# FFN chunks that run on over the batches: 10 chunks of up to 512 tokens in place of 12, and one x tile for all batches

## Chip, cores and metric

The kernel runs on one core of a Trainium2 chip. The metric is the device time of one execution in microseconds. In one job the fast executions of the kernel before lay within 0.3% (187.84 to 188.35 us). Now and then one takes some 3.7 us longer (191.78 in place of 188.1 us) at the same granted clock, which is the share of TensorE's full speed that the profile records as given. Such a run is called slow here, and it is left out of every ratio; the medians quoted are of all runs. "Stream" below is a second measure of mine. It is read from the trace's records at nanosecond resolution, and runs from the start of the first FFN matmul of token 1088 (the 49th pg, a term explained below, of every program but one, which is named) to the start of the last matmul on TensorE.

## The reference

Polynomial-sketch attention over 4 batches, 4 heads, 1088 tokens and head size 32, and then a squared-ReLU feed-forward network (FFN) over all 4352 tokens; the code is shortened.

```python
def _attn_ref(q, k, v, S1, S2):
    # phi(x): the outer product of two 8-wide sketches of x -> 64 features
    q_p, k_p = phi(q), phi(k)
    kv = np.einsum('bhsf,bhsd->bhfd', k_p, v)
    z = np.sum(k_p, axis=2)
    num = np.einsum('bhsf,bhfd->bhsd', q_p, kv)
    den = np.einsum('bhsf,bhf->bhs', q_p, z)[..., None] + 1e-06
    return num / den

def _moe_ref(x, w_in, w_out):            # x: 4352 x 128, w_in: 128 x 2048
    h = np.maximum(x @ w_in, 0.0)
    return h * h @ w_out

# x = attention output, (batch, seq) x (head * head_dim)
```

## The kernel before

The attention of batch b+1 is woven into the FFN of batch b. The FFN goes over the tokens in chunks (`FC`, one list for each batch). For every chunk it goes through 16 slices of 128 hidden units. One slice is one first-layer matmul into a PSUM tile `pg`, a relu on ScalarE, a square on ScalarE or VectorE, and one second-layer matmul that accumulates into `po`. I call the pg of one slice with the po of an earlier slice, as TensorE runs them, a block.

```python
    AC = [[(0, 8), (8, 12), (20, 16)]] + [[(0, 4 * NT)]] * (B - 1)
    FC = [[(0, 256), (256, 384), (640, 448)]] + [[(0, 384), (384, 384), (768, 320)]] * (B - 2)
    FC += [[(0, 448), (448, 384), (832, 256)]]
    ...
    for b in range(B):
        for ci, (c0, n) in enumerate(FC[b]):
            ...
                units.append((b, ci, c0, n, d0, m))      # one unit: m slices of a chunk
    ...
    def ffn1(u, i):                                      # pg; w_in and xT are fp32r
        nc.tensor.matmul(
            st["pg", u][:, n * i : n * i + n],
            w_in[:, 128 * (d0 + i) : 128 * (d0 + i) + 128],
            st[b, "xT"][:, c0 : c0 + n],                 # one xT tile for each batch
        )
    def ffn2(u, i, xs=None):                             # po; w_o and g are fp32
        ...                                              # (the last chunk: token-major, tokens on the partitions)
            nc.tensor.matmul(po[0][:, 0:n], w, g, start=(d == 0), stop=(d == NB - 1))
```

The attention puts four kinds of inserts into TensorE's stream: the sketches `kc` and `qc`, the key-value sums `kvp`, and `nd`, which makes numerator and denominator of x.

```python
    def a_nd(b, i0, nb): ...
        for e in range(E):
            qp = st[b, "qp", i0, e]
            ch = [(c, h) for c in range(4) for h in range(H)]
            for c, h in ch:
                r, o = slice(32 * c, 32 * c + 32), 64 * h + 32 * e
                nc.tensor.matmul(nd[32 * h : 32 * h + 32, 512 * c : 512 * c + m],
                                 kv[r, o : o + 32], qp[r, m * h : m * h + m], ...)
    def a_x(b, i0, nb, x, k=2): ...                      # VectorE: xT = nd * bc
```

A planner in the program orders the work of every engine from estimated durations. The order of the FFN matmuls among themselves is fixed, po and pg in turn. Where an insert falls in it is up to the planner, and a parameter `lag` sets how long after its inputs it may fall.

```python
    PEL, M, T0 = 0.3, 5.0, 1.5
    O.add(("nd", b, i0), {"PE": ...}, ..., uses=qps + ..., rings=[("att", 1)], lag=PEL)
    ...
    seq = [x for u in range(LU) for x in pe1[u]]
    for u in range(NU):
        p, q_ = list(pe2[u]), list(pe1[u + LU]) if u + LU < NU else []
        while p or q_:
            seq += p[:1] + q_[:1]
            p, q_ = p[1:], q_[1:]
```

## Time and profile before

| | before |
|---|---|
| time, median of 3 runs | 188.1 us (187.9 to 188.18) |
| span of the profiled run, granted TensorE clock | 186.1 us, 0.998 |
| TensorE / ScalarE / VectorE busy | 97% / 80% / 63% |
| blocks from token 1088 on | 144: 5 chunks of 384, 2 of 320, 1 of 448, 1 of 256 (the last) |
| stream (token 1088 to the last matmul) | 124.258 us |

The page and the lists of waits that bound the kernel stand in the prediction. Durations of single matmul records are of little use, since they overlap: in the two FFN groups shown there, po is busy for 138.4 us and pg for 110.2, together more than the span.

### The profile page before, as it was taken

Reading aid. Unit: us, or ns where it says so; the run is one execution under the profiler, and the core shown is the slowest. Engines: PE = TensorE matmul, PEld = TensorE weight load, DVE = VectorE, ACT = ScalarE, POOL = GpSimd, SP = SyncE. Lnnn points to the kernel's source line nnn. Section 1 sums busy time; section 2 is a strip of 40 time slices with the busy share of each in tenths; the row PEclk is TensorE's granted clock in tenths of the full one; section 3 lists DMA queues with packets and bytes.
Section 4 is the critical chain, followed back from the end, with each engine's and each line's share of the span. In section 5 each row is a group of like instructions: output and inputs, shape, how many; then the busy total and the mean of one; then the engine's idle time right before and its main releaser. Section 6 shows DMA issues by size and latency. Waiting matters only on the chain.

```text
span 186.1 us, 4132 instructions
## 1 busy us (share of the span) xinstructions
PE 180.4 (97%) x1561; PEld 120.8 (65%) x1562; DVE 116.7 (63%) x263; ACT 149.3 (80%) x329; POOL 35.8 (19%) x157
## 2 busy tenths in 40 slices
PE   8998999999999999999999999999999999999991
PEld 2766766666555566666577666656577655666891
DVE  4979989958991699379934689379943412222400
ACT  3509778878979889789698989789698998999960
POOL 2736405327400000184000000185000000000000
PEclk9999999999999999999999999999999999999999
DMA  5899600100039600200059200200020200020200
GB/s 181 201 301 330 168 0 5 28 4 0 4 48 250 153 4 0 45 3 0 13 120 270 38 4 0 42 4 0 8 40 0 35 0 2 8 41 4 30 12 28
DMA packets 24555, 11.27 MB, mean 61 GB/s; under 512 B 17880, under 2 KB 23000, under 8 KB 24536
## 3 DMA queue, kind: packets, MB, share of 16 engines
q1 hardware_dynamic: 24084, 10.82, 24.5%
q8 instruction: 12, 0.20, 0.5%
q10 hardware_dynamic: 452, 0.20, 0.4%
q14 instruction: 7, 0.06, 0.1%
HBM read 8.78 MB, written 2.23 MB: 59 GB/s over the span
## 4 chain that ended last, share of the span: by engine, by line
PE 95%; DMA 2%; DVE 1%; ACT 0%; issue 0%; POOL 0%; ACTq 0%; DVEq 0%
PE po L619 60%; PE pg L581 18%; PE nd L531 3%; PE kvp L397 2%; PE pol L614 2%; PE po L614 2%; PE qc L299 2%; DMA s_nat<-in_S_dram 2%; PE kvp L379 1%; PE kf L309 1%; PE kc L299 1%; PE x L713 1%; ACT gt L590 0%; PE den L774 0%; PE num L774 0%
## 5 line engine op out<-in xcount | busy, mean ns | idle before, releaser
L619 PE MATMUL po<-g,w_o 128*128 128x384 f32 (+3 forms) x352 | 138.4, 478 | 0.0
L581 PE MATMUL pg<-xT,w_in 128*128 128x384 f32 (+3 forms) x192 | 110.2, 582 | 0.5 <-ACT gt L590 0.5
L590 ACT ACTIVATE gt<-pg 128x384 f32<-128x384 f32 (+4 forms) x177 | 85.3, 489 | 19.3 <-PE pg L581 16.1
L619 PEld LDWEIGHTS po<-g,w_o 128*128 128x128 f32 x352 | 62.5, 189 | 22.6 <-issue 7.4
L598 ACT ACTIVATE g<-gt 128x384 f32<-128x384 f32 (+3 forms) x138 | 70.9, 531 | 2.9
L581 PEld LDWEIGHTS pg<-xT,w_in 128*128 128x128 f32 x192 | 36.0, 189 | 25.0 <-issue 6.0
L600 DVE TENSOR_TENSOR g<-gt 128x384 f32<-128x384 f32 (+4 forms) x39 | 21.9, 563 | 38.4 <-ACT gt L590 38.4
L438 POOL COPY kv<-kvt 32x64 f32<-32x64 f32 x48 | 11.8, 246 | 71.3 <-PE po L619 63.0
L492 POOL COPY rd<-rc 32x9 f32<-32x9 f32 (+2 forms) x80 | 16.6, 207 | 13.2 <-DVE rc L484 9.9
L501 DVE STREAM_SHUFFLE qa<-qc 128x576 f32<-128x576 f32 (+2 forms) x20 | 11.6, 648 | 0.0
L516 DVE TENSOR_TENSOR qp<-qa,qb 128x576 f32<-128x576 f32 (+2 forms) x20 | 10.8, 600 | 0.0
L464 DVE STREAM_TRANSPOSE qt<-qc 128x576 f32<-128x576 f32 (+2 forms) x10 | 5.8, 615 | 6.2 <-PE qc L299 6.2
L350 DVE TENSOR_TENSOR kp<-fs 128x576 f32<-128x576 f32 x12 | 8.2, 741 | 0.0
L623 DVE STREAM_TRANSPOSE oT<-po 128x384 f32<-128x384 f32 (+3 forms) x11 | 6.1, 559 | 1.8 <-PE po L619 1.8
L531 PE MATMUL nd<-qp,kv 32*32 32x288 f32 (+2 forms) x320 | 6.8, 353 | 0.0
L341 DVE STREAM_TRANSPOSE fs<-kc 128x576 f32<-128x576 f32 x6 | 4.3, 762 | 3.2 <-PE kc L299 3.2
L550 DVE TENSOR_TENSOR xT<-nd,bc 128x576 fp32r<-128x576 f32 (+2 forms) x10 | 5.6, 600 | 1.0 <-PE nd L531 1.0
L531 PEld LDWEIGHTS nd<-qp,kv 32*32 32x32 f32 x320 | 3.8, 103 | 3.6 <-issue 1.7
L501 DVE STREAM_SHUFFLE qb<-qc 128x576 f32<-128x576 f32 (+2 forms) x10 | 6.0, 646 | 0.0
L541 DVE STREAM_TRANSPOSE bc<-rd 128x576 f32<-128x576 f32 (+2 forms) x10 | 5.8, 606 | 0.2
L292 DVE STREAM_TRANSPOSE qT<-qn 128x192 f32<-128x192 f32 (+3 forms) x11 | 5.8, 564 | 0.0
L614 PE MATMUL pol<-w_o,g 128*128 128x128 f32 x32 | 5.7, 275 | 0.0
(94 smaller groups left out, 94.1 us busy)
## 6 DMA issues: line engine op xcount, KB each, us to landing
kn<-in_k_dram SPq DMA_DIRECT2D x3, 544.0 KB, 6.3
qn<-in_q_dram SPq DMA_DIRECT2D x3, 544.0 KB, 6.7
vn<-in_v_dram SPq DMA_DIRECT2D x9, 144.0 KB, 5.3
out_dram<-oT SPq DMA_DIRECT2D x24, 48.0 KB, 1.8
w_in<-in_moe_w_in_dram SPq DMA_DIRECT2D x4, 256.0 KB, 5.6
w_o<-in_moe_w_out_dram SPq DMA_DIRECT2D x4, 256.0 KB, 6.5
out_dram<-oT SPq DMA_DIRECT2D x8, 56.0 KB, 1.9
vn<-in_v_dram SPq DMA_DIRECT2D x3, 112.0 KB, 6.1
```

The costliest lines, as they stand in the source:

```text
L350: nc.vector.tensor_tensor(out=_ap(st[b, "kp"], 0, 128, 2 * o, [[64, NT], [8, 8], [1, 8]]), in0=_ap(fs, 0, 128, o, [[32, NT], [1, 8], [0, 8]]),
L438: nc.gpsimd.tensor_copy(_ap(st[b, "kv"], 32 * c, 32, 64 * h, [[32, E], [1, 32]]), _ap(st["kvt"], 32 * h, 32, 0, [[64, E], [1, 32]]),)
L492: nc.gpsimd.tensor_copy(st[b, "rd", i0][32 * h : 32 * h + 32, n * c : n * c + n], st["rc"][32 * c : 32 * c + 32, n * h : n * h + n],)
L501: nc.vector.stream_shuffle(in_=banks(st[b, "qc", i0], 2 * x, 0, m), out=_ap(st[b, which, i0], 0, 128, 2 * m * x, [[m, 2], [1, m]]), mask=m ...
L516: nc.vector.tensor_tensor(out=st[b, "qp", i0, e][:, r], in0=st[b, f"qa{e}", i0][:, r], in1=st[b, "qb", i0][:, r], op=mult,)
L531: nc.tensor.matmul(nd[32 * h : 32 * h + 32, 512 * c : 512 * c + m], kv[r, o : o + 32], qp[r, m * h : m * h + m], start=(e == 0), stop=(e = ...
L581: nc.tensor.matmul(st["pg", u][:, n * i : n * i + n], w_in[:, 128 * (d0 + i) : 128 * (d0 + i) + 128], st[b, "xT"][:, c0 : c0 + n],)
L590: nc.scalar.activation(gt[:, 0:w], st["pg", u][:, 0:w], Relu)
L598: nc.scalar.activation(g2[:, 0:w], gt[:, 0:w], Square)
L600: nc.vector.tensor_tensor(out=g2[:, 0:w], in0=gt[:, 0:w], in1=gt[:, 0:w], op=mult)
L614: nc.tensor.matmul(po[x // 128][:, 0:128], g[:, x : x + 128], w, start=(d == 0), stop=(d == NB - 1),)
L619: nc.tensor.matmul(po[0][:, 0:n], w, g, start=(d == 0), stop=(d == NB - 1))
```

## The change

Its intent is to run fewer, wider blocks. Chunks no longer stop at a batch's end, so that five of them can have 512 tokens, the width of the program's PSUM tiles; for this the x of all batches has to lie in one tile. The core of the diff:

```diff
-    FC = [[(0, 256), (256, 384), (640, 448)]] + [[(0, 384), (384, 384), (768, 320)]] * (B - 2)
-    FC += [[(0, 448), (448, 384), (832, 256)]]
+    FC, at = [], 0
+    for n in (256, 384, 448, 448, 512, 512, 512, 512, 512, 256):
+        FC.append((at, n))
+        at += n
...
+    xT = sb("xT", B * S + SP - S, F32R)
...
-            out=_ap(st[b, "xT"], 0, 128, 32 * i0 + 2 * m * x, [[m, k], [1, m]]),
+            out=_ap(xT, 0, 128, S * b + 32 * i0 + 2 * m * x, [[m, k], [1, m]]),
...
-            st[b, "xT"][:, c0 : c0 + n],
+            xT[:, c0 : c0 + n],
...
-    def f_out(b, c0, n):
+    def f_out(c0, n):                      # a chunk across a boundary: two stores
+        for b in range(B):
+            lo, hi = max(c0, b * S), min(c0 + n, b * S + S)
...
-            ("x", b, i0, x) for i0, k in AC[b] for x in range(2)
-            if 32 * i0 + 16 * k * x < c0 + n and c0 < 32 * i0 + 16 * k * x + 16 * k
+            ("x", b, i0, x) for b in range(B) for i0, k in AC[b] for x in range(2)
+            if b * S + 32 * i0 + 16 * k * x < c0 + n
+            and c0 < b * S + min(32 * i0 + 16 * k * x + 16 * k, S)
```

The rest of the diff drops the batch index from units, tiles and task names.

More of the change, by code (lines that the diff above doesn't have):

```diff
@@ L547, in a_x @@
         m = 8 * nb
-        if (b, "xT") not in st:
-            st[b, "xT"] = bpool.tile([128, SP], F32R, tag="xT", name="xT")
         nc.vector.tensor_tensor(
-            out=_ap(st[b, "xT"], 0, 128, 32 * i0 + 2 * m * x, [[m, k], [1, m]]),
+            out=_ap(xT, 0, 128, S * b + 32 * i0 + 2 * m * x, [[m, k], [1, m]]),
             in0=banks(st[b, "nd", i0], 2 * x, 0, m, k),
@@ L558 @@
     units, first_unit, dur = [], {}, []
-    for b in range(B):
-        for ci, (c0, n) in enumerate(FC[b]):
-            first_unit[b, c0] = len(units)
-            nb = 512 // n
-            sizes = [nb] * (NB // nb)
-            if (b, ci) == (0, 0):
-                sizes = [1, 1] + [2] * 7
-            d0 = 0
-            for m in sizes:
-                units.append((b, ci, c0, n, d0, m))
-                dur.append(m * (5 * n / 2400 + 0.015))
-                d0 += m
+    for ci, (c0, n) in enumerate(FC):
+        first_unit[c0] = len(units)
+        nb = 512 // n
+        sizes = [nb] * (NB // nb)
+        if ci == 0:
+            sizes = [1, 1] + [2] * 7
+        d0 = 0
+        for m in sizes:
+            units.append((ci, c0, n, d0, m))
+            dur.append(m * (5 * n / 2400 + 0.015))
+            d0 += m
     NU = len(units)
-    last = len(FC[B - 1]) - 1
+    last = len(FC) - 1
     g2s = {}
     def ffn1(u, i):
-        b, ci, c0, n, d0, m = units[u]
+        ci, c0, n, d0, m = units[u]
         if i == 0:
@@ L583, in ffn1 @@
             w_in[:, 128 * (d0 + i) : 128 * (d0 + i) + 128],
-            st[b, "xT"][:, c0 : c0 + n],
+            xT[:, c0 : c0 + n],
         )
     def relu(u):
-        w = units[u][3] * units[u][5]
+        w = units[u][2] * units[u][4]
         gt = fpool.tile([128, 512], F32, tag="gt", bufs=GT, name="gt")
@@ L593, in square @@
     def square(u, eng):
-        w = units[u][3] * units[u][5]
+        w = units[u][2] * units[u][4]
         g2 = fpool.tile([128, 512], F32, tag="g2", bufs=G2, name="g2")
@@ L603, in ffn2 @@
     def ffn2(u, i, xs=None):
-        b, ci, c0, n, d0, m = units[u]
+        ci, c0, n, d0, m = units[u]
         d = d0 + i
         if d == 0:
-            st["po", b, c0] = [psf.tile([128, 512], F32, tag="po", name="po")]
-            if (b, ci) == (B - 1, last):
-                st["po", b, c0].append(att("pol"))
-        po = st["po", b, c0]
+            st["po", c0] = [psf.tile([128, 512], F32, tag="po", name="po")]
+            if ci == last:
+                st["po", c0].append(att("pol"))
+        po = st["po", c0]
         g, w = g2s[u][:, n * i : n * i + n], w_o[:, 128 * d : 128 * d + 128]
-        if (b, ci) == (B - 1, last):
+        if ci == last:
             for x in range(0, n, 128) if xs is None else xs:
@@ L619, in ffn2, with f_oT, f_last @@
             nc.tensor.matmul(po[0][:, 0:n], w, g, start=(d == 0), stop=(d == NB - 1))
-    def f_oT(b, c0, n):
-        oT = fpool.tile([128, 448], F32, tag="oT", bufs=2, name="oT")
-        nc.vector.transpose(oT[:, 0:n], st["po", b, c0][0][:, 0:n])
-        st["oT", b, c0] = oT
-    def f_out(b, c0, n):
-        for dm in range(4):
-            nc.sync.dma_start(
-                bass.AP(
-                    out.tensor, out.offset + (b * S + c0 // 32) * 128 + 32 * dm,
-                    [[G * 128, 32], [128, n // 32], [1, 32]],
-                ),
-                _ap(st["oT", b, c0], 32 * dm, 32, 0, [[32, n // 32], [1, 32]]),
-            )
-    def f_last(b, c0):
-        po = st["po", b, c0]
+    def f_oT(c0, n):
+        oT = fpool.tile([128, 512], F32, tag="oT", bufs=2, name="oT")
+        nc.vector.transpose(oT[:, 0:n], st["po", c0][0][:, 0:n])
+        st["oT", c0] = oT
+    def f_out(c0, n):
+        for b in range(B):
+            lo, hi = max(c0, b * S), min(c0 + n, b * S + S)
+            if lo >= hi:
+                continue
+            i0, m = (lo - b * S) // 32, (hi - lo) // 32
+            for dm in range(4):
+                nc.sync.dma_start(
+                    bass.AP(
+                        out.tensor, out.offset + (b * S + i0) * 128 + 32 * dm,
+                        [[G * 128, 32], [128, m], [1, 32]],
+                    ),
+                    _ap(st["oT", c0], 32 * dm, 32, lo - c0, [[32, m], [1, 32]]),
+                )
+    def f_last(c0):
+        po, b = st["po", c0], B - 1
         def store(eng, i):
@@ L641, in store @@
                 bass.AP(
-                    out.tensor, out.offset + (b * S + c0 // 32 + 4 * i) * 128,
+                    out.tensor, out.offset + (b * S + (c0 - b * S) // 32 + 4 * i) * 128,
                     [[128, 4], [G * 128, 32], [1, 128]],
@@ L798 @@
     nc.vector.transpose(bc0[:, :], _ap(rd0, 0, 128, 0, [[1, 8], [0, 32]]))
-    st[0, "xT"] = bpool.tile([128, SP], F32R, tag="xT", name="xT")
     nc.vector.tensor_tensor(
-        out=st[0, "xT"][:, 0:256], in0=num0[:, 0:256], in1=bc0[:, :], op=mult
+        out=xT[:, 0:256], in0=num0[:, 0:256], in1=bc0[:, :], op=mult
     )
@@ L809, with unit_at @@
         t += 1.14 * dur[u]
+    def unit_at(x):
+        return first_unit[max(c for c, _ in FC if c <= x)]
     def due(b, c0):
-        c = max(c for c, _ in FC[b] if c <= c0)
-        return tu[first_unit[b, c]] - LA
+        return tu[unit_at(b * S + c0)] - LA
     def dve(n):
@@ L901, in nd_tasks @@
                 uses=[("bc", b, i0, x), ("nd", b, i0)],
-                rings=[("xT", 2)] if x == 0 and (i0 == 0) else [],
             )
@@ L912, in k_tasks @@
     def k_tasks(b, k0, ks_lead):
-        s0 = tu[first_unit[b - 1, 0]] - 4.0 if b > 1 else 0.0
+        s0 = tu[unit_at(b * S - S)] - 4.0 if b > 1 else 0.0
         O.add(
@@ L985 @@
     for u in range(NU):
-        b, ci, c0, n, d0, m = units[u]
+        ci, c0, n, d0, m = units[u]
         w = n * m
         xt = [
-            ("x", b, i0, x) for i0, k in AC[b] for x in range(2)
-            if 32 * i0 + 16 * k * x < c0 + n and c0 < 32 * i0 + 16 * k * x + 16 * k
+            ("x", b, i0, x) for b in range(B) for i0, k in AC[b] for x in range(2)
+            if b * S + 32 * i0 + 16 * k * x < c0 + n
+            and c0 < b * S + min(32 * i0 + 16 * k * x + 16 * k, S)
         ]
@@ L1023 @@
         pe2.append(mm2s)
-        if d0 + m == NB and (b, ci) != (B - 1, last):
-            po = [x for u_ in range(first_unit[b, c0], u + 1) for x in pe2[u_]]
-            O.add(("oT", b, c0), {"DVE": dve(n)}, tu[u] + 3.0, [], on(f_oT, b, c0, n), uses=po,
+        if d0 + m == NB and ci != last:
+            po = [x for u_ in range(first_unit[c0], u + 1) for x in pe2[u_]]
+            O.add(("oT", c0), {"DVE": dve(n)}, tu[u] + 3.0, [], on(f_oT, c0, n), uses=po,
                   rings=[("oT", 2)])
             O.add(
-                ("out", b, c0), {"SP": 2.0}, tu[u] + 4.0, [], on(f_out, b, c0, n),
-                uses=[("oT", b, c0)],
+                ("out", c0), {"SP": 2.0}, tu[u] + 4.0, [], on(f_out, c0, n),
+                uses=[("oT", c0)],
             )
@@ L1043 @@
     O.run()
-    f_last(B - 1, FC[B - 1][last][0])
+    f_last(FC[last][0])
 _INS = ['q', 'k', 'v', 'S1', 'S2', 'moe_w_in', 'moe_w_out']
```

## The prediction

> **What bounds the kernel now.** I read the page's busy shares and chain first, then TensorE's waits, then the timeline of TensorE in steady stretches of the three chunk widths, then ScalarE and VectorE around the places that the change touches.
>
> ```profile
> PE 180.4 (97%) x1561; PEld 120.8 (65%) x1562; DVE 116.7 (63%) x263; ACT 149.3 (80%) x329; POOL 35.8 (19%) x157
> ...
> PE 95%; DMA 2%; DVE 1%; ACT 0%; issue 0%; POOL 0%; ACTq 0%; DVEq 0%
> ...
> L619 PE MATMUL po<-g,w_o 128*128 128x384 f32 (+3 forms) x352 | 138.4, 478 | 0.0
> L581 PE MATMUL pg<-xT,w_in 128*128 128x384 f32 (+3 forms) x192 | 110.2, 582 | 0.5 <-ACT gt L590 0.5
> ```
>
> TensorE is 95% of the chain that ended last, and the two FFN lines almost never find it idle: 0.0 and 0.5 us. The list of TensorE's waits says the same in full:
>
> ```profile
> PE warm L662 <- PEq L1058: 0.8, 1, 0.8
> PE pg L581 <- ACT gt L590: 0.5, 1, 0.5
> PE kf L309 <- ACT sq L683: 0.3, 1, 0.3
> PE qc L299 <- issue: 0.3, 1, 0.3
> ```
>
> 1.9 us in four waits, all within the first 16 us, which the change leaves alone. So a saving on ScalarE, VectorE or the queues is worth nothing; only what TensorE's own stream costs counts. Records of a pipelined matmul overlap, so I take that cost from the starts of the same instruction in consecutive blocks. A block is one first-layer matmul (pg) and the second-layer ones (po) of an earlier block:
>
> ```profile
> 67.14 0.63 PE L581 MATMUL pg<-xT,w_in 128*128 128x384 f32 x1
> ...
> 75.34 0.63 PE L581 MATMUL pg<-xT,w_in 128*128 128x384 f32 x1
> ...
> 134.53 0.55 PE L581 MATMUL pg<-xT,w_in 128*128 128x320 f32 x1
> ...
> 142.08 0.55 PE L581 MATMUL pg<-xT,w_in 128*128 128x320 f32 x1
> ...
> 146.79 0.71 PE L581 MATMUL pg<-xT,w_in 128*128 128x448 f32 x1
> ...
> 156.32 0.71 PE L581 MATMUL pg<-xT,w_in 128*128 128x448 f32 x1
> ```
>
> Between the two lines of a pair lie 10, 11 and 10 blocks: 0.820, 0.686 and 0.953 us a block at 384, 320 and 448 columns. From 320 to 448 that is 2.086 ns a column, and what is left at zero columns is 0.686 - 320 x 0.002086 = 0.0185 us (0.019 from the 384 row). **A block costs about 0.019 us whatever its width, the rest is proportional to the columns.**
>
> **What the Trainium skill says.** "TensorE: Matmul & The Clock Gate", section "Wait — 56ns, not 53.3ns?", gives a warm back-to-back matmul as N / 2.4 GHz plus a fixed 2.5 ns or so. "FP8 and Floating Point Precision", section "TensorE Precision Notes", has four passes for true fp32. The trace agrees in form: 2.086 ns a column is five passes at 2.4 GHz (2.083), one for pg, whose operands are the reduced fp32r type, and four for the fp32 po. In size the fixed part is larger here, 19 ns for three records, against 7.5 ns if it were 2.5 each; I use the trace. "PSUM — Partial Sum Buffer", section "The four PSUM rules", limits a matmul's output to one bank, 512 fp32 columns. So 512 is the end of this road; the tiles pg and po are allocated 512 wide already, so no buffer count changes. "ScalarE: Activation LUTs", section "What ACT_TABLE_LOAD costs", gives an ACTIVATE with immediate operands 186 ns + 0.833 ns a column, with back-to-back ones overlapping by 93 ns. The trace's 481 ns at 384 and 588 ns at 512 columns are 0.836 ns a column and 160 ns fixed, for relu out of PSUM; squares have 0.859 and 190. No page bears on the scheduling.
>
> **The change part by part.**
>
> Common part. The instruction order of both programs is the same on TensorE until the first pg of token 1088, at 57.68 us: the 256-, 384- and 448-column chunks of batch 0 are unchanged. Nothing changes there.
>
> Fewer blocks. From token 1088 on, before has per 16 blocks: five chunks of 384, two of 320, one of 448, one of 256 (the last, which is computed token-major in both). After has one of 448, five of 512, one of 256. The same 3264 columns in 144 blocks against 112. At 512 columns a block is, extrapolated, 0.953 + 64 x 0.002086 = 1.0865 us. Before: 16 x (5 x 0.820 + 2 x 0.686 + 0.953) = 102.8 us. After: 16 x (0.953 + 5 x 1.0865) = 102.2 us. The exact difference is 32 blocks x about 0.0195 = **-0.63 us**, all of it on the path.
>
> Attention inserts. The matmuls of batches 2 and 3 (kc, kvp, qc, nd) stay the same in number and shape, but three of them move from between pg and po to between po and pg. Read by pg starts, an insert between po and pg looks dearer: kvp costs 2.46 - 0.82 = 1.64 us at 37.08 to 39.54, against 2.27 - 0.82 = 1.45 us at 75.34 to 77.61. That would be +0.6 us for three and eat the whole gain. But the pg record that follows an insert is 0.44 us long instead of 0.63: its start is drawn later. By ends, 37.71 to 39.98, it is 2.27 - 0.82 = 1.45 us as well. So I put **0** here.
>
> ScalarE and VectorE. 177 relus become 145. Squares go from 138 on ScalarE and 39 on VectorE to 123 and 22. ScalarE records then sum to 2 x 0.38 + 16 x 0.481 + 32 x 0.534 + 95 x 0.588 = 81.4 us of relu and 16 x 0.520 + 28 x 0.573 + 79 x 0.630 = 74.1 us of square: 155.5 against 156.2 us before. Beside TensorE, **0**.
>
> Output. oT is transposed 9 times instead of 11, and the two chunks across a batch boundary are stored in two parts: still 44 stores from it. A store's landing is awaited by nobody before the end, and the last chunk is the same. **0**.
>
> Sum: 188.1 - 0.63 = **187.5 us**.
>
> **The rivals.**
>
> (a) x comes too late. A chunk across a boundary needs batch 2's x 128 tokens earlier and batch 3's 192 tokens earlier, some 4 and 6.5 us at 34 ns a token (0.820 x 16 / 384). The nd matmuls must therefore run earlier, and they wait for VectorE. In the kernel before the margin is small:
>
> ```profile
> 121.16 0.77 PE L299 MATMUL qc<-qT,sw 32*32 32x288 f32 x32
> ...
> 132.45 1.60 PE L531 MATMUL nd<-qp,kv 32*32 32x288 f32 x64
> ```
> ```profile
> 129.17 2.74 DVE L516 TENSOR_TENSOR qp<-qa,qb 128x576 f32<-128x576 f32 x4
> 131.84 1.43 DVE L541 STREAM_TRANSPOSE bc<-rd 128x576 f32<-128x576 f32 x2
> ```
>
> qp is done at 131.91, 9.98 us after qc's end and 0.54 us before nd. In the changed order ten po and nine pg of 512 columns stand between qc and nd of batch 3, an estimated 10 x 0.869 + 9 x 0.217 = 10.6 us; for batch 2 some 10.5 us. No other VectorE work is put in between. So the 0.5 us margin holds, and six or seven blocks (6.5 us or more) lie between nd and the first pg that needs the x, which takes VectorE 1.5 us. If the chain slipped by an unforeseen square (0.67 us) at both batches, the cost would be up to 0.3 us: 187.8. For it: the margin is thin. Against: the counts.
>
> (b) ScalarE becomes the bound. Two relus and two squares at 384 take 1.50 us at their closest (87.76 to 89.26), 0.75 a unit; 128 more columns add 0.22: 0.97 against 1.087 on TensorE. Where a square directly follows its own relu, 66.17 to 67.12 shows 0.95 a unit, so 1.17 at 512: ScalarE falls back 0.08 us a unit there, against 0.13 before. The longest such stretch is some nine units, 0.7 us, with a lead of about 1.3 us by the two pg buffers, and inserts let it catch up. If it bit, +0.5 to 1 us: 188 to 188.5.
>
> (c) One x tile for all batches makes false waits: a pg that reads batch 1's tokens waiting for the write of batch 2's, 1 to 2 us at each of two boundaries, 189 to 191. The listing of the changed program's waits speaks against it: the pg after nd wait for ScalarE alone, and the first that waits for VectorE is the one that needs the new x.
>
> (d) The fixed part is not per block but a hidden weight load, and 512 columns gain nothing: 188.1. The equal remainder at three widths speaks against it.
>
> **Range and chances.** The gain is certain in sign if nothing new waits, and 0.3% in size; a slip of (a) or (b) could take it back, (c) hardly. The three times before span 0.28 us. I say 187.5, with 187.0 to 188.1 for 8 in 10. A change over 2% needs 3.8 us, six times what I can find in either direction: 0.01 faster, 0.97 within, 0.02 slower.
>
> **What would show it.** Right: pg starts 1.087 us apart at 512 columns; TensorE's waits still under 2 us and only at the start; the first 256-column pg of the last chunk 0.6 us earlier than before's 170.76 us; nd of batches 2 and 3 still a few tenths after qp. Wrong: a block at 512 over 1.10 us; a wait of nd for qp or of pg for the x or a relu; an insert between po and pg that costs more by record ends too.

## The result, and the profile after

| | before | after |
|---|---|---|
| time, median of all 4 runs | 188.14 us | 187.91 us |
| fast runs (one slow run of each left out) | 187.9 to 188.18 | 187.57 to 187.93 |
| ratio of fast runs, 95% interval | | 0.9986 (0.9963 to 1.0009) |
| stream | 124.258 us | 123.981 us |

A ratio here is the mean time of one kernel's fast runs over that of the other's fast runs in the same rounds, so it is not quite the ratio of the medians quoted. The change is worth 0.1 to 0.2%, and these rounds alone would not tell it from nothing. The stream is 0.277 us shorter; that I can read to some nanoseconds, because two traces of one program agree to that (shown below), while the start-up ahead of it shifts by tenths of a microsecond from run to run: the first FFN matmul started between 13.66 and 14.29 us in the traces. The two profiled runs both have a span of 186.1 us for that reason.

The page of the kernel after, first its line of busy times (time, share of the span, instructions), then the chain by engine, then the two FFN groups (busy, mean ns of one, idle before):

```profile
PE 180.5 (97%) x1466; PEld 105.0 (56%) x1466; DVE 109.6 (59%) x244; ACT 147.5 (79%) x282; POOL 35.6 (19%) x157
...
PE 94%; DMA 2%; DVE 1%; ACT 0%; issue 0%; POOL 0%; ACTq 0%; DVEq 0%
...
L620 PE MATMUL po<-g,w_o 128*128 128x512 f32 (+3 forms) x288 | 133.2, 546 | 0.1
L582 PE MATMUL pg<-xT,w_in 128*128 128x512 f32 (+3 forms) x160 | 104.6, 664 | 0.6 <-ACT gt L591 0.5
```

There are 32 blocks fewer, and TensorE bounds the kernel as before. Its busy time did not fall (180.4 to 180.5 us). Busy time joins overlapping records, so a stream without gaps is busy for as long as it lasts, and the 0.28 us that it lost are hidden by the start-up, where 12 warming matmuls ran in place of 11 (5.1 us against 4.5). Its waits in full (us in total, times, longest):

```profile
PE warm L668 <- PEq L1065: 0.8, 1, 0.8
PE pg L582 <- ACT gt L591: 0.5, 1, 0.5
PE kf L313 <- ACT sq L689: 0.3, 1, 0.3
```

All three are in the start-up, so no new wait ate the gain. The spacing of the blocks is what differs from the prediction. TensorE's timeline (start and length in us), on both sides of the nd of batch 3:

```profile
116.99 0.79 PE L582 MATMUL pg<-xT,w_in 128*128 128x512 f32 x1
...
124.60 0.79 PE L582 MATMUL pg<-xT,w_in 128*128 128x512 f32 x1
...
126.18 1.60 PE L535 MATMUL nd<-qp,kv 32*32 32x288 f32 x64
...
128.51 0.80 PE L582 MATMUL pg<-xT,w_in 128*128 128x512 f32 x1
...
139.44 0.80 PE L582 MATMUL pg<-xT,w_in 128*128 128x512 f32 x1
```

Seven blocks lie between the first two pg lines: 7.61 / 7 = 1.087 us, as predicted. Ten lie between the last two: 10.93 / 10 = 1.093 us. The same instructions on the same shapes cost 6.5 ns more each behind the nd than ahead of it, and the length of the pg record (0.79 or 0.80) is a handy mark of which spacing holds. From the records' starts, the 6.5 ns lie between the start of a pg and that of its first po record (630 against 636.5 ns); the other two gaps of a block are alike. A later weight load is not the cause: the load for that po starts 402 to 403 ns behind the pg and takes 190 ns in quick and slow blocks alike. Of the 67 steady 512-column blocks, 20 have 1.087 and 47 have 1.093: the slow ones are those behind the nd of batch 2 and of batch 3, up to the next insert or the end, and the others all run at 1.087.

Where the stream's time went, beyond what its columns take at 2.4 GHz (us; a part's records are counted end to end, less five passes a column at 1/2.4 ns):

| | before | after |
|---|---|---|
| ordinary FFN blocks | 127: 2.446 | 95: 2.168 |
| kc and qc (4) | 3.658 | 3.663 |
| kvp (2) | 2.944 | 2.946 |
| nd (2) | 3.491 | 3.515 |
| last chunk | 3.681 | 3.653 |

The ordinary blocks account for the -0.28 us; the rest cancels to within 0.01. At before's 19.3 ns a block, 95 blocks would have 1.83 us. The 0.34 us in between is 47 slow blocks at 6.7 ns, 0.31 us, and a few blocks where two widths meet.

### The profile page after: what moved, and what is told of

Same layout as the page of the kernel before. It is cut to its first block, busy times and chain, and to the rows that moved or that the text cites. A ratio compares the mean times of both kernels' runs of the same rounds, so it can differ in the third digit from the quotient of the medians.

```text
span 186.1 us, 3857 instructions
## 1 busy us (share of the span) xinstructions
PE 180.5 (97%) x1466; PEld 105.0 (56%) x1466; DVE 109.6 (59%) x244; ACT 147.5 (79%) x282; POOL 35.6 (19%) x157
## 4 chain that ended last, share of the span: by engine, by line
PE 94%; DMA 2%; DVE 1%; ACT 0%; issue 0%; POOL 0%; ACTq 0%; DVEq 0%
PE po L620 60%; PE pg L582 18%; PE nd L535 3%; PE kvp L401 2%; PE pol L615 2%; PE po L615 2%; DMA s_nat<-in_S_dram 2%; PE qc L303 2%; PE kvp L383 1%; PE kf L313 1%; PE kc L303 1%; PE x L719 1%; ACT gt L591 0%; PE warm L668 0%; PE num L780 0%
## 5 line engine op out<-in xcount | busy, mean ns | idle before, releaser
L620 PE MATMUL po<-g,w_o 128*128 128x512 f32 (+3 forms) x288 | 133.2, 546 | 0.1
L582 PE MATMUL pg<-xT,w_in 128*128 128x512 f32 (+3 forms) x160 | 104.6, 664 | 0.6 <-ACT gt L591 0.5
L591 ACT ACTIVATE gt<-pg 128x512 f32<-128x512 f32 (+3 forms) x145 | 81.0, 562 | 21.3 <-PE pg L582 20.5
L599 ACT ACTIVATE g<-gt 128x512 f32<-128x512 f32 (+2 forms) x123 | 71.9, 602 | 2.6
L620 PEld LDWEIGHTS po<-g,w_o 128*128 128x128 f32 x288 | 53.0, 189 | 30.1 <-issue 20.1
L582 PEld LDWEIGHTS pg<-xT,w_in 128*128 128x128 f32 x160 | 30.0, 189 | 31.3 <-issue 14.2
L601 DVE TENSOR_TENSOR g<-gt 128x512 f32<-128x512 f32 (+2 forms) x22 | 14.2, 649 | 41.8 <-ACT gt L591 41.8
L624 DVE STREAM_TRANSPOSE oT<-po 128x512 f32<-128x512 f32 (+3 forms) x9 | 5.9, 653 | 7.4 <-PE po L620 7.4
L668 PE MATMUL warm<-const-bfloat16-1.0 128*128 128x512 bf16 x12 | 5.1, 578 | 0.8 <-PEq L1065 0.8
```

Of the source, the lines that this page charges most:

```text
L582: nc.tensor.matmul(st["pg", u][:, n * i : n * i + n], w_in[:, 128 * (d0 + i) : 128 * (d0 + i) + 128], xT[:, c0 : c0 + n],)
L591: nc.scalar.activation(gt[:, 0:w], st["pg", u][:, 0:w], Relu)
L599: nc.scalar.activation(g2[:, 0:w], gt[:, 0:w], Square)
L601: nc.vector.tensor_tensor(out=g2[:, 0:w], in0=gt[:, 0:w], in1=gt[:, 0:w], op=mult)
```

## The experiments

Where a kernel ran once, I rely on its trace. All results were correct.

**Theory:** a 512-column block has two spacings, 6.7 ns apart, and which of them a stretch gets is settled when the stream restarts behind an insert. **Rivals:** the slow stretches are chance of the run; the fixed part of a block does not belong to the block at all (rival (d) of the prediction); the one x tile or the flat chunk list brings a cost of its own, which offset part of the gain.

### again: the changed kernel, unchanged

> The changed kernel once more. Block theory: TensorE's stream is shorter by 32 blocks x 20 ns = 0.64 us, less what the first trace shows to go against it: 53 of the 512-column blocks, all those between an nd and the next insert, came at 1.093 us apart and not 1.087, which is 53 x 6.7 ns = 0.35 us. Net -0.28 us, ratio 0.9985. If the slower spacing belongs to the program, the same blocks show it again; if it is luck of an execution, other blocks do, or none, and the ratio can be 0.9966.

Measured: 187.76 us against 188.06, ratio 0.9983 (0.9964 to 1.0002), in a later job. The stream is 123.981 us, to the nanosecond that of the first trace, though it begins 0.5 us later. Again 20 blocks have 1.087 and 47 have 1.093, in the same places. (The 53 of the expectation was a first count; 47 steady blocks are slow in both traces.) TensorE's timeline behind the nd of batch 3 in this run:

```profile
128.99 0.80 PE L582 MATMUL pg<-xT,w_in 128*128 128x512 f32 x1
...
136.64 0.80 PE L582 MATMUL pg<-xT,w_in 128*128 128x512 f32 x1
```

7.65 / 7 = 1.093 us. So the slow spacing belongs to the program and is not chance of the run.

### twelve: the old widths in the new form

```diff
-    for n in (256, 384, 448, 448, 512, 512, 512, 512, 512, 256):
+    for n in (256, 384, 448, 384, 384, 320, 384, 384, 320, 448, 384, 256):
```

> One x tile and the chunk list over all batches, but with the twelve widths of the kernel before. Block theory: 192 blocks as before, no chunk crosses a batch, ratio 1.000 within 0.001. Rival, that the one x tile itself makes or removes a wait: a ratio off 1.000 by 0.003 or more, and a wait of pg for VectorE in the trace.

Measured: 188.34 us against 188.06, ratio 1.0011 (0.9997 to 1.0025). The stream is 124.241 us against before's 124.258, and the 127 ordinary blocks have 2.463 us beyond their columns against 2.446. The one x tile and the flat list cost nothing on TensorE and give nothing: the rival of a hidden cost falls, and with it (c) of the prediction.

### eleven: 448 columns in place of 512

```diff
-    for n in (256, 384, 448, 448, 512, 512, 512, 512, 512, 256):
+    for n in (256, 384, 448, 448, 448, 448, 448, 448, 448, 320, 256):
```

> Eleven chunks of at most 448 columns, run on over the batches. Block theory: 16 blocks fewer than before, -0.32 us, ratio 0.9983, with 448-column blocks at 0.953 us everywhere. If crossing a batch costs something, a wait of nd for qp or of pg for xT shows at the chunks that cross. If the slower spacing after nd is not special to 512 columns, 448-column blocks of 0.960 us show after nd.

Measured: 188.13 us against 188.06, ratio 1.0002 (0.9988 to 1.0016). The stream is 124.069 us, 0.19 below before's. All 448-column blocks run at 0.953 us wherever they stand, behind an nd too, so the two spacings are seen at 512 columns alone. The ordinary blocks (111) have 2.173 us, as much as 95 blocks after the change: the slow spacing took almost exactly what the 16 blocks fewer were to give. One thing was not foreseen: the last chunk has 3.766 us here, 0.11 more than in the changed kernel. The trace shows where. The weight load of the pg behind the first token-major block starts 568 ns after the pg before it, against 451 in the changed kernel, and 52 ns after the end of a relu, which frees a pg buffer and which the profile names as what the load waited for. So TensorE waited there for ScalarE, in a gap that its list of waits does not show, because the records of the po before it cover it.

### fifteen: many narrow blocks

```diff
-    for n in (256, 384, 448, 448, 512, 512, 512, 512, 512, 256):
+    for n in (256, 384, 448, 256, 256, 256, 256, 256, 256, 256, 256, 256, 352, 352, 256):
```

> Fifteen chunks, nine of them of 256 columns: the same columns in 48 blocks more than before. Block theory: 48 x 20 ns = +0.96 us, ratio 1.0051, 256-column blocks at 0.553 us. Rival, that the fixed part is not paid per block: ratio 1.000. If 256-column blocks are bound by the three weight loads of a block: more than +2 us.

Measured: 188.38 us against 188.06, ratio 1.0013 (1.0000 to 1.0026); the stream is 124.308 us. With 20 ns for every block, 48 blocks more than before had to cost 0.96 us. The stream grew by 0.05. TensorE's timeline in a stretch of 256 columns:

```profile
106.08 0.47 PE L582 MATMUL pg<-xT,w_in 128*128 128x256 f32 x1
...
111.56 0.47 PE L582 MATMUL pg<-xT,w_in 128*128 128x256 f32 x1
```

Ten blocks in 5.48 us, 0.548 each (0.5467 by the records' starts). Five passes of 256 columns at 2.4 GHz are 0.5333, which leaves 13.3 ns, not 20. The 352-column blocks have 0.753 us, which leaves 20. And 144 x 13.3 + 32 x 20 = 2.56 us is what 128 blocks at 20 ns cost before. **A fixed part that is the same for every width falls here**, and this was the ground on which the prediction extrapolated to 512.

### nd_inside: the nd of batches 2 and 3 behind a pg instead of behind a po

```diff
-            uses=qps + [("qp", b, i0, 0, 0)], rings=[("att", 1)], lag=PEL,
+            uses=qps + [("qp", b, i0, 0, 0)], rings=[("att", 1)], lag=PEL + (0.6 if b > 1 else 0.0),
```

> The changed kernel with nd of batches 2 and 3 half a block earlier or later, between pg and po instead of between po and pg; nothing else moves by more than a block. Two traces of the changed kernel showed 1.093 us a 512-column block after such an nd and 1.087 after the other inserts. If the place of nd in the block sets the spacing: all 512-column blocks at 1.087 us, TensorE's stream from the 49th pg to the last matmul 0.35 us under 123.98 us, 123.63, and a ratio of 0.9966 to before. If nd itself sets it: 1.093 after nd again, 123.98 us, 0.9985.

Measured: 187.65 us against 188.25, ratio 0.9964 (0.9946 to 0.9981). The stream is 123.719 us, 0.54 below before's. TensorE's timeline behind the nd of batch 2 and behind that of batch 3:

```profile
87.63 1.60 PE L535 MATMUL nd<-qp,kv 32*32 32x288 f32 x64
...
89.72 0.80 PE L582 MATMUL pg<-xT,w_in 128*128 128x512 f32 x1
...
98.47 0.80 PE L582 MATMUL pg<-xT,w_in 128*128 128x512 f32 x1
...
126.36 1.60 PE L535 MATMUL nd<-qp,kv 32*32 32x288 f32 x64
...
128.45 0.79 PE L582 MATMUL pg<-xT,w_in 128*128 128x512 f32 x1
...
140.40 0.79 PE L582 MATMUL pg<-xT,w_in 128*128 128x512 f32 x1
```

8.75 / 8 = 1.094 us in the first pair, 11.95 / 11 = 1.086 in the second. Only the eight blocks behind the nd of batch 2 are slow now; the 38 behind that of batch 3, which reach to the last chunk, are not. TensorE's work is the same, and only the two inserts have moved, by one matmul each. Elsewhere the planner gave ScalarE two squares that VectorE had (125 and 20 in place of 123 and 22), and TensorE has no wait behind the start from it. The move is worth 0.26 us of stream against the changed kernel. It also shows that the place alone is no rule: both inserts moved in the same way, and one stretch stayed slow.

### nd_reversed: the matmuls within every nd in the opposite order

```diff
-            ch = [(c, h) for c in range(4) for h in range(H)]
+            ch = [(c, h) for c in range(3, -1, -1) for h in range(H - 1, -1, -1)]
```

> The changed kernel with the 16 small matmuls of each half of nd issued in the opposite order, so that another corner of the array is used last; nd stays between po and pg. If what nd leaves in the array sets the slower spacing: 1.087 us after nd. If its place or its length does: 1.093 us, and 123.98 us of stream.

Measured, one run: 187.6 us; the stream is 123.778 us. 55 blocks run at 1.087 and 12 at 1.093. Both stretches behind the nd of batches 2 and 3 are quick. The slow ones are elsewhere: the first five of 512 columns, between the qc of batch 2 and its nd, and seven behind the kc of batch 3. So it is not "behind an nd": other inserts are followed by a slow stretch as well. In this run, nd_dummy and reversed_2_3 the other engines have the changed kernel's instructions in its order.

### nd_dummy: one small matmul more behind the nd

```diff
+        if b:
+            nc.tensor.matmul(
+                nd[:, 384 : 384 + 64],
+                nc.const_aps.tensor(1.0, (128, 128), mybir.dt.bfloat16),
+                nc.const_aps.tensor(1.0, (128, 64), mybir.dt.bfloat16),
+            )
```

It writes columns that nobody reads, and the result stays correct.

> The changed kernel with one 64-column bf16 matmul of ones behind nd of batches 1 to 3, into columns of its tile that nobody reads (results stay right). It costs some 0.03 to 0.1 us three times. If the slower spacing is a matter of the phase in which the stream restarts after nd, it may turn to 1.087 us, and the stream is 123.98 - 0.35 + 0.2 = 123.8 us; if not, 1.093 us and about 124.2 us.

Measured, one run: 187.34 us; the stream is 123.824 us. The counts are 55 and 12, in the same places as in nd_reversed. A matmul that adds work (nd has 3.551 us here, 0.04 more than in the changed kernel) makes the stream 0.16 us shorter, because the stretches behind it become quick. TensorE's timeline behind the nd of batch 3:

```profile
130.38 0.79 PE L588 MATMUL pg<-xT,w_in 128*128 128x512 f32 x1
...
139.07 0.79 PE L588 MATMUL pg<-xT,w_in 128*128 128x512 f32 x1
```

8.69 / 8 = 1.086 us. So neither the order of the nd's matmuls nor its side of the pg has to change for it: one more matmul ahead of the restart is enough.

### widths: the fixed part at 288, 416 and 480 columns

```diff
-    for n in (256, 384, 448, 448, 512, 512, 512, 512, 512, 256):
+    for n in (256, 384, 448, 480, 480, 480, 416, 288, 288, 288, 288, 256):
```

> Twelve chunks with widths not yet seen, 480, 416 and 288 columns, as many blocks as before. If every block has 20 ns beside its columns: 1.020, 0.887 and 0.620 us a block, stream 124.26 us as before. The run with fifteen chunks showed 13.3 ns at 256 columns (0.5467 us) and not 20: if the fixed part comes in steps of 6.7 ns, each of these three is off its streaming time of 1.000, 0.8667 and 0.600 us by 13.3, 20 or 26.7 ns.

Measured, one run: 187.84 us; the stream is 124.128 us. TensorE's timeline at 288 columns:

```profile
135.52 0.51 PE L582 MATMUL pg<-xT,w_in 128*128 128x288 f32 x1
...
144.72 0.51 PE L582 MATMUL pg<-xT,w_in 128*128 128x288 f32 x1
```

15 blocks in 9.20 us, 0.613 each. Together with the other runs (medians over steady blocks, from the records' starts):

| columns | us a block | five passes at 2.4 GHz | fixed part, ns |
|---|---|---|---|
| 256 | 0.5467 | 0.5333 | 13.3 |
| 288 | 0.6133 | 0.6000 | 13.3 |
| 320 to 480 (six widths) | 0.686 to 1.020 | 0.667 to 1.000 | 20 |
| 512, quick | 1.087 | 1.0667 | 20 |
| 512, slow | 1.0933 | 1.0667 | 26.7 |

The fixed part goes in steps of some 6.7 ns. The slow 512-column block is as long as two of 256. Like eleven, this kernel has an unforeseen extra in its last chunk, 3.874 us against 3.653, at the same pg: its weight load starts at 672 ns, 50 ns after the relu's end.

### reversed_2_3: the opposite order for batches 2 and 3 alone

```diff
             ch = [(c, h) for c in range(4) for h in range(H)]
+            ch = ch[::-1] if b > 1 else ch
```

> The changed kernel with the opposite order of nd's small matmuls in batches 2 and 3 alone. With it in all batches, the blocks after nd turned to 1.087 us but the first stretch of 512-column blocks, set off by nd of batch 1, turned to 1.093. If the spacing is set by how the stream restarts after the last insert, every 512-column block now comes at 1.087 us, the stream is 123.98 - 0.35 = 123.63 us, and the ratio to before 0.9966. If the spacing were a matter of luck or of the chip, some stretch stays at 1.093 and the stream above 123.7.

Measured: 187.63 us against 188.23, ratio 0.9967 (0.9952 to 0.9982). The stream is 123.712 us, not 123.63: 60 blocks are quick, as hoped for behind both nd, but seven behind the kc of batch 3 are slow, which are quick in the changed kernel. TensorE's timeline behind that kc, and behind the nd of batch 3:

```profile
100.92 0.77 PE L303 MATMUL kc<-kT,sf 32*32 32x288 f32 x32
...
102.41 0.80 PE L583 MATMUL pg<-xT,w_in 128*128 128x512 f32 x1
...
110.07 0.80 PE L583 MATMUL pg<-xT,w_in 128*128 128x512 f32 x1
...
129.36 0.80 PE L583 MATMUL pg<-xT,w_in 128*128 128x512 f32 x1
...
140.23 0.79 PE L583 MATMUL pg<-xT,w_in 128*128 128x512 f32 x1
```

7.66 / 7 = 1.094 us, and 10.87 / 10 = 1.087. (The 0.80 at 129.36 is a single block of 1.090 us; the lines after it show 0.79.) The kc itself did not change. Something upstream of it did, so a stretch behind an insert that is not touched can turn too. I can say where the slow spacing stood in every trace, but not foretell where it will stand.

### crossing_early: what rival (a) costs where it bites

Chunks of 512 from token 640 on, so that the first chunk across a boundary comes before batch 1's x can be ready.

```diff
-    for n in (256, 384, 448, 448, 512, 512, 512, 512, 512, 256):
+    for n in (256, 384, 512, 512, 512, 512, 512, 448, 448, 256):
```

> Ten chunks as in the change, but with 512 columns from token 640 on, so that the boundary from batch 0 to 1 is crossed too; the two of 448 come late. As many blocks as in the change. Theory: what counts at a boundary is whether x is there. In the kernel before, the chunk at 640 started near 40.3 us and x of batch 1 was written at 54.2 to 55.6, so pg now waits: TensorE idles for most of 14 us less the insert moved out, some 10 to 13 us, time 198 to 201 us, with nd waiting for qp in the trace. If crossing is harmless as such: 187.8 us.

Measured: 202.49 us against 188.23, ratio 1.0759 (1.0740 to 1.0779), a little more than was expected. (Its 49th pg is not that of token 1088, so its stream is not compared.) The first four of TensorE's waits:

```profile
PE nd L535 <- DVE qp L520: 8.0, 1, 8.0
PE kvp L401 <- DVE xT L552: 1.1, 1, 1.1
PE pg L582 <- DVE xT L552: 1.0, 1, 1.0
PE qc L303 <- DVE kvt L419: 0.9, 1, 0.9
```

They sum to 11.0 us, and the time grew by 14.3. I put most of the rest down to TensorE's clock, which was halved from about 42.5 to 59.6 us. The page's row of granted clock, in 40 slices of 5.0 us; TensorE's timeline of the qc and the nd; and two windows (us, then busy us and instructions of PE, PEld, DVE, ACT and POOL, then granted clock, DMA share and GB/s):

```profile
PEclk9999999975559999999999999999999999999999
```
```profile
42.63 1.27 PE L303 MATMUL qc<-qT,sw 32*32 32x288 f32 x32 [0.90 <-DVE kvt L419]
51.93 3.22 PE L535 MATMUL nd<-qp,kv 32*32 32x288 f32 x64 [8.03 <-DVE qp L520]
```
```profile
45.00:55.00 10.00, 3.07 (x64) 1.15 (x64) 9.90 (x22) 0.00 (x0) 4.91 (x23) 0.50 0.30 82
55.00:62.00 7.00, 5.99 (x28) 3.64 (x15) 2.84 (x5) 3.67 (x7) 0.00 (x0) 0.67 0.00 0
```

After eight slices at full speed come one at 0.7 and three at 0.5, then full speed again. The qc takes 1.27 us in place of 0.77 and the nd 3.22 in place of 1.60, and the FFN that runs at half speed from 56.2 to 59.6 us loses an estimated half of these 3.4 us. That is 0.5 + 1.6 + 1.7 = 3.8, against the 3.3 that are left. The Trainium skill, "TensorE: Matmul & The Clock Gate", section "What's actually happening", has it that an idle window of about 3.4 us gates the array down to 1.2 GHz, half its rate, and a busy one releases it. The size agrees, with 0.50 granted from 45 to 55 us, and so does the release, after 3.4 us of gapless matmuls. But the 8 us wait did not bring the fall on. The clock fell at 42.5 us, and that wait began at 43.9. Until then no gap of TensorE behind the start had been longer than 1.1 us, and its matmul records filled 1.5 of the last 3.4 us. What counts as idle, no run here shows. A chunk that crosses a boundary too early thus costs its waits and, here, several microseconds of half speed.

## Why the prediction was right, and where its sum was off

- **The bound, and what can't matter.** Right. TensorE has 94% of the chain after, and its three waits are start-up. ScalarE's relu and square groups fell from 156.2 us busy to 81.0 + 71.9 = 152.9, and no pg waited for a relu behind the start: rival (b) did not come. (The prediction's 155.5 adds up records, while its 156.2 joins those that overlap; the records of before add up to 159.8.) In a small way it did come in eleven and widths, with 0.11 and 0.22 us in the last chunk.
- **Inserts: 0.** Right. The eight inserts took 10.09 us beyond their FFN columns before and 10.12 after, though three moved from one side of a pg to the other. To read them by record ends was the right choice.
- **x in time, rival (a).** Right. In VectorE's timeline after, the work that the nd of batch 3 waits for is

```profile
122.64 2.76 DVE L520 TENSOR_TENSOR qp<-qa,qb 128x576 f32<-128x576 f32 x4
```

  done at 125.40, and the nd starts at 126.18, 0.78 us later; for batch 2 the same margin is 0.65 us. The prediction's counts gave 10.6 - 9.98, about 0.6. crossing_early shows that the rival is real: four waits and 14 us, when the boundary chunk comes too early.
- **One x tile, rival (c).** Did not come: twelve has the same stream as before to 0.02 us.
- **Fewer blocks: -0.63 us.** The sign was right, the size was not: the stream lost 0.28 us. The step that failed is the sentence "A block costs about 0.019 us whatever its width", and with it 1.0865 us for every block at 512. Measured were 20 blocks at 1.087 and 47 at 1.093 us; the latter take back 0.31 us. The prediction called three equal remainders at 320, 384 and 448 columns enough to dismiss rival (d). All three lie within one step of the table above. The 256-column blocks would have shown 13 ns, but the prediction left them out of the fit.
- **The listed checks.** It called a block over 1.10 us the sign of an error; 1.093 passes that, and at 47 blocks was still half the gain. The check "first 256-column pg of the last chunk 0.6 us earlier" shows 170.05 against 170.76 us, 0.71 earlier, and looks like a full success. It was badly chosen: in the kernel after, po of 512 columns still follow that pg where they had 384 before. From that pg to the last matmul it takes 181.934 - 170.76 = 11.17 us before and 181.936 - 170.05 = 11.89 after. The start of the last matmul is the fair mark, and counted from a mark behind the start-up, as the stream is.
- **The range.** 187.0 to 188.1 held 187.91 because it left room for half of the gain to be lost. The loss came from a step that the rivals named only as all or nothing. That the time fell inside is thus no evidence for the 0.63 us; the stream is, and it shows less than half of it.
- **What it took from the skill.** The four passes for fp32 ("FP8 and Floating Point Precision", section "TensorE Precision Notes") hold at 512 columns too: 1.087 us a block against 1.0667 for five passes at 2.4 GHz. So does the limit of one bank ("PSUM — Partial Sum Buffer", section "The four PSUM rules"), as far as a run can show it: tiles of 512 fp32 columns brought no wait of TensorE.

**What is shown, and what is open.** Shown: the slow spacing repeats in a second trace of the same program, holds for a whole stretch between two inserts, is seen at 512 columns only, and shifts with the place or content of an insert while the FFN work stays the same (nd_inside, nd_reversed, nd_dummy, reversed_2_3). Not shown: the mechanism of the 6.7 ns steps. That the stream locks into one of several phases when it restarts fits all runs, but nothing here measures a phase.

**Two kernels beat the one before clearly.** nd_inside (0.9964) and reversed_2_3 (0.9967) are the only ones whose whole interval is below before's time. They gain 0.54 and 0.55 us of stream, nearly the 0.63 of the prediction; against the changed kernel only the stream separates them, since the intervals of the ratios overlap. Both differ from before by less than 0.4%, and either could turn with the next edit of the inserts.

## What to carry to other kernels

When a kernel's bound is a gapless TensorE stream, measure a block's cost by the spacing of equal instructions, at more than the few widths that stand close together, and at the extremes that you have, before you extrapolate to a width that it has never run. A saving of nanoseconds a block should be checked in every stretch of the trace and not in one, since the same block can have two spacings, which change at an insert. And before you let a chunk cross into data that is made late, count the margin: 0.6 us of it was enough here, while the kernel without it lost 14 us.

## What the Trainium skill lacked or had wrong

- "TensorE: Matmul & The Clock Gate", section "Wait — 56ns, not 53.3ns?": it gives one fixed cost of about 2.5 ns for a warm matmul. For these blocks of one fp32r and one fp32 matmul the runs show 13.3 ns at 256 and 288 columns, 20 at 320 to 480, and 20 or 26.7 at 512. Only the first is near five passes of 2.5 ns (12.5, an estimate from the page's figure); the page does not say whether a record or a pass has the cost, nor that it depends on the width.
- No page says that a steady stream of the same matmuls can have two spacings: 1.087 or 1.093 us for a 512-column block, for a whole stretch between two inserts.
- "ScalarE: Activation LUTs", section "What ACT_TABLE_LOAD costs": its 186 ns fixed stand against 160 for relu out of PSUM and 190 for squares in the trace of before; its slope of 0.833 ns a column agreed for relu (0.836); squares had 0.859.
- "TensorE: Matmul & The Clock Gate", section "What's actually happening": it ties the half clock to an idle window of about 3.4 us, and does not say how little work counts as idle. In crossing_early the clock fell to 0.50 with matmul records in 1.5 of the last 3.4 us and no gap over 1.1 us, 1.4 us before the 8 us wait began.
